# Two contraction tiles of the first tokens by plain loads and TensorE transposes, the other three by one DMA transpose, with all loads on SyncE's queue

## The chip, the core and the metric

The kernel runs on one core of a Trainium2 chip. The metric is device time in microseconds (us), as the median of several executions. The profile that is quoted is of one execution, taken by the hardware profiler; its span runs from the first to the last instruction of the program.

## What is computed

A feed-forward block without biases, all in bf16, with accumulation in float32:

```python
B, S, D, F = 1, 2048, 640, 1728
# x: (B, S, D), w1: (D, F), w2: (F, D)
h = jnp.einsum("bsd,df->bsf", x, w1)
h = silu(h)
out = jnp.einsum("bsf,fd->bsd", h, w2)
```

## The kernel before

TensorE contracts over the 128 partitions. The first product has its contraction over D = 640, which makes five contraction tiles, numbered 0 to 4. F = 1728 is thirteen blocks of 128 columns and a last one of 64. The 2048 tokens are four chunks of 512. The first product is made transposed, with w1 as the stationary operand and x, transposed to `xT` (features on partitions, tokens along the row), as the moving one, so each matmul of a block and a chunk is 128x512 and fills one of the eight PSUM banks after five contraction tiles. ScalarE applies SiLU from PSUM into `hT`. The second product takes `hT` as its operand, most of it with w2 moving; its results are evicted by VectorE and ScalarE in turn and stored by SP. The 64 last columns of F, and the last 128 columns of D in the second product, have paths of their own late in the kernel.

The program is written engine by engine, with semaphores by hand: `wait` puts a wait on an engine ahead of its next instruction, `tick` lets an instruction raise a semaphore. Each engine keeps the order in which the code issues to it. `ahead_of_start` moves what it issues ahead of the barrier at the program's start, and `barrier_wait_here` moves an engine's wait at that barrier to the place of the call. So the order of the first microseconds is that of the code, per engine.

What matters here is chunk 0, the first 512 tokens:

- x must reach `xT` transposed. `turned` does that with a DMA transpose from HBM, `first(i)` for the pairs of tiles in `KT`, which is tiles 1 and 2, and then 3 and 4. Tile 0 goes another way: `xk` is loaded as it stands (tokens on partitions), TensorE transposes its four 128x128 blocks against `ident` into banks 6 and 7, and VectorE copies them to `xT`.
- w1 comes in slabs. `load_k` (called by `slab`) loads the first `FA` = 8 blocks of one contraction tile, 256 KB; `half` loads half of such a slab. Slabs of tiles 0 and 1 come as halves. ScalarE's queue issues two of the four halves, after it has waited for the first two dummies. All other loads are SP's. Blocks 8 to 12 and the last 64 columns follow in two loads for all five tiles (`FG`).
- `dummies` are matmuls on zeros in bank 3: nine ahead of the transposes and one behind them.
- `k_pass(k, fts, a, e)` runs contraction tile k over the blocks `fts`. For chunk 0 the loop over k is outside and that over the eight blocks inside, so eight banks are open at once, and tile k needs only its own part of x and its own slab. Tile 0 starts with four blocks in half width (256 tokens each).
- The blocks from 8 on, and chunks 1 to 3, have the loop over k inside. Their x comes by DMA transposes of two, two and one tile, behind the start's loads in SP's queue.

In the profile every matmul through `mm`, in both products, has line L221. Plain loads and stores are L89, DMA transposes of x L122, dummies L146, TensorE's transposes L195, the copies out of them L197, SiLU L225.

Of the kernel before, what the change touches and what calls it, by code (L numbers as in the profile page):

```python
# [9 lines left out]
def bass_standalone__dense_activation_silu__prompt_kernel(  # L10
# [6 lines left out]
    bf16 = mybir.dt.bfloat16  # L17
# [6 lines left out]
    P = 128  # L24
    NB = 8
    BANK = 512
    DT = D // P
    FT = F // P
    FL = F - FT * P
    SCH = 512  # L30
    HB = 256
# [6 lines left out]
    pe, act, dve, pool, sp = nc.tensor, nc.scalar, nc.vector, nc.gpsimd, nc.sync  # L38

    with ExitStack() as es:  # L40
        def sb(name, shape, dtype):
            return es.enter_context(nc.sbuf_tensor(name, shape, dtype))

        xT = sb("xT", [P, DT, S], bf16)
# [4 lines left out]
        hTt = sb("hTt", [P, NSC // 2, SCH], bf16)  # L49
        oT = sb("oT", [P, S], bf16)  # L50
        o_sb = sb("o_sb", [P, S // P, D], bf16)
        xk = sb("xk", [P, SCH // P, P], bf16)
        ident = sb("ident", [P, P], bf16)
        warm = sb("warm", [P, 32], fp32)
        z = sb("z", [P, HB], bf16)
        ps = es.enter_context(nc.psum_tensor("ps", [P, NB, BANK], fp32))
# [4 lines left out]
        def sem(name):  # L61
            s = es.enter_context(nc.semaphore(name))
            count[s.name if hasattr(s, "name") else name] = 0
            return [s, 0]

        def tick(ins, s, n=1):
            ins.then_inc(s[0], n)
            s[1] += n
            return (s, s[1])

        def wait(eng, *points):
            for pt in points:
                if pt is None:
                    continue
                s, v = pt
                key = (id(eng), id(s))
                if seen.get(key, 0) < v:
                    eng.wait_ge(s[0], v)
                    seen[key] = v

        s_pe, s_act, s_dve = sem("s_pe"), sem("s_act"), sem("s_dve")
# [4 lines left out]
        def load(eng, out_ap, in_ap):  # L86
            s = sem(f"s_ld{n_dma[0]}")
            n_dma[0] += 1
            return tick(eng.dma_start(out=out_ap, in_=in_ap), s, 16)  # L89

        ET = mybir.EngineType

        def preamble(engine, opcode):
            lst = nc.main_func.blocks[0].instructions
            return next(
                i for i, ins in enumerate(lst)
                if ins.opcode == opcode and ins.engine == engine
            )

        def ahead_of_start(emit, engine):  # L100
            lst = nc.main_func.blocks[0].instructions
            n = len(lst)
            r = emit()
            lst = nc.main_func.blocks[0].instructions
            new = lst[n:]
            del lst[n:]
            at = preamble(engine, "Drain")
            lst[at:at] = new
            return r

        def barrier_wait_here(engine):
            lst = nc.main_func.blocks[0].instructions
            lst.append(lst.pop(preamble(engine, "EventSemaphore")))
# [4 lines left out]
        FA = 8  # L118
        FG = [(8, 11), (11, FT)]

        def turned(c, k0, k1, s):
            return tick(sp.dma_start_transpose(  # L122
                out=xT[:, k0:k1, c * SCH:(c + 1) * SCH],
                in_=xf[c * SCH:(c + 1) * SCH, k0 * P:k1 * P],
            ), s, 16)

        def load_k(eng, k):
            return load(eng, w1s[:, k, 0:FA * P], w1_v[:, k, 0:FA * P])

        ld_w1 = {}  # L130
        KT = [(1, 3), (3, DT)]
        s_x = [sem(f"s_x{k0}") for k0, _ in KT]
        ld_x = {}

        def first(i):
            k0, k1 = KT[i]
            pt = turned(0, k0, k1, s_x[i])
            for k in range(k0, k1):
                ld_x[k] = pt
        p_z = ahead_of_start(lambda: tick(dve.memset(z[:, :], 0.0), s_dve), ET.DVE)  # L140
        x_v = xf.rearrange("(j p) d -> p j d", p=P)
        bank_free = [None] * NB

        def dummies(n):
            for _ in range(n):
                ins = pe.matmul(ps[:, 3, 0:HB], lhsT=z[:, 0:P], rhs=z[:, :], start=True, stop=True)  # L146
            return tick(ins, s_pe)
# [9 lines left out]
        FH = FA // 2  # L157
        ld_k = {}

        def slab(k):  # L160
            ld_k[k] = load_k(sp, k)

        def half(eng, k, h):
            a, b = (0, FH * P) if h == 0 else (FH * P, FA * P)
            return load(eng, w1s[:, k, a:b], w1_v[:, k, a:b])

        p_ident = ahead_of_start(identity, ET.Pool)
        ld_xk = ahead_of_start(lambda: load(sp, xk[:, :, :], x_v[:, 0:SCH // P, 0:P]), ET.SP)
        ld_a = {}
        ld_a[0] = ahead_of_start(lambda: half(sp, 0, 0), ET.SP)  # L170
        wait(pe, p_z)
        wait(act, dummies(2))
        ld_k[0] = half(act, 0, 1)
        ld_a[1] = half(act, 1, 0)
        ahead_of_start(lambda: first(0), ET.SP)
        ld_k[1] = ahead_of_start(lambda: half(sp, 1, 1), ET.SP)
        ahead_of_start(lambda: slab(2), ET.SP)
        first(1)
        slab(3)
        slab(4)  # L180
        for a, b in FG:
            e = F if b == FT else b * P
            pt = load(sp, w1s[:, :, a * P:e], w1_v[:, :, a * P:e])
            for ft in range(a, b):
                ld_w1[ft] = pt
        barrier_wait_here(ET.SP)
        barrier_wait_here(ET.Activation)

        dummies(7)
        wait(pe, ld_xk, p_ident)  # L190
        turned0 = []
        for h in range(2):
            v = ps[:, 6 + h, :].bitcast(bf16)
            for i in range(2):
                ins = pe.transpose(v[:, i * P:(i + 1) * P], xk[:, 2 * h + i, :], ident[:, :])  # L195
            wait(dve, tick(ins, s_pe))
            r = tick(dve.tensor_copy(  # L197
                out=xT[:, 0, h * HB:(h + 1) * HB], in_=v[:, 0:HB]), s_dve)
            bank_free[6 + h] = r
            turned0.append(r)  # L200
        dummies(1)
        barrier_wait_here(ET.DVE)

        p_warm = tick(pool.memset(warm[:, :], 0.0), s_pool)
# [15 lines left out]
        def mm(o, l, r, start, stop, shared=False):  # L220
            return pe.matmul(o, lhsT=l, rhs=r, start=start, stop=stop, skip_group_check=shared)  # L221

        def silu(out_ap, in_ap, bank, after):
            wait(act, after)
            r = tick(act.activation(out=out_ap, in_=in_ap, func=ACT.Silu), s_act)  # L225
            bank_free[bank] = r
            return r

        def k_pass(k, fts, a=0, e=SCH):
            for ft in fts:  # L230
                if k == 0:
                    wait(pe, bank_free[ft])
                ins = mm(ps[:, ft, a:e], w1s[:, k, ft * P:(ft + 1) * P], xT[:, k, a:e],
                         start=(k == 0 and a == 0), stop=(k == DT - 1), shared=True)
                if k == DT - 1:
                    silu(hT[:, ft, 0:SCH], ps[:, ft, :], ft, tick(ins, s_pe))

        wait(pe, ld_a[0], turned0[0])
        k_pass(0, range(FH), 0, HB)
        wait(pe, turned0[1])  # L240
        k_pass(0, range(FH), HB, SCH)
        wait(pe, ld_k[0])
        k_pass(0, range(FH, FA))
        wait(pe, ld_x[1], ld_a[1])
        k_pass(1, range(FH))
        wait(pe, ld_k[1])
        k_pass(1, range(FH, FA))
        barrier_wait_here(ET.PE)
        for k in range(2, DT):
            wait(pe, ld_x[k], ld_k[k])  # L250
            k_pass(k, range(FA))

        nxt = [FA]

        def bank():
            b = nxt[0] % NB
            nxt[0] += 1
            wait(pe, bank_free[b])
            return b

        for ft in range(FA, FT):
            wait(pe, ld_w1[ft])
            b = bank()
            for k in range(DT):
                ins = mm(ps[:, b, :], w1s[:, k, ft * P:(ft + 1) * P], xT[:, k, 0:SCH],
                         start=(k == 0), stop=(k == DT - 1))
            silu(hT[:, ft, 0:SCH], ps[:, b, :], b, tick(ins, s_pe))
        for c in range(1, NSC):
            wait(pe, ld_xc[c])
            for ft in range(FT):  # L270
                b = bank()
                for k in range(DT):
                    ins = mm(ps[:, b, :], w1s[:, k, ft * P:(ft + 1) * P],
                             xT[:, k, c * SCH:(c + 1) * SCH], start=(k == 0), stop=(k == DT - 1))
                h_last = silu(hT[:, ft, c * SCH:(c + 1) * SCH], ps[:, b, :], b, tick(ins, s_pe))
        h_tail = []
        for q in range(NSC // 2):
            b = bank()
            for k in range(DT):
                for hh in range(2):  # L280
                    c = 2 * q + hh
                    ins = mm(ps[hh * FL:(hh + 1) * FL, b, :], w1s[:, k, F0:F],
                             xT[:, k, c * SCH:(c + 1) * SCH],
                             start=(k == 0), stop=(k == DT - 1), shared=True)
# [85 lines left out]
        for c in range(NSC):  # L370
            b = bank()
# [5 lines left out]
        for q in range(NSC // 2):  # L377
# [6 lines left out]
            for hh in range(2):  # L384
                c = 2 * q + hh
                r = evac(oT[:, c * SCH:(c + 1) * SCH], ps[:, wbank[c], :], wbank[c], tt[hh])
                wait(sp, r)
                st_w[c] = tick(sp.dma_start_transpose(
                    out=o_sb[:, c * JB:(c + 1) * JB, DA:D],
                    in_=oT[:, c * SCH:(c + 1) * SCH],  # L390
# [36 lines left out]
```

## Time and profile before

| What | us |
|---|---|
| median of 6 runs | 125.22 |
| lowest and highest run | 124.79, 125.67 |
| the profiled execution | 125.17 |
| its span | 123.8 |
| TensorE matmuls, busy | 120.0 |
| TensorE weight loads, busy | 55.1 |
| ScalarE, busy | 38.1 |
| VectorE, busy | 8.1 |

The page lists, for each group of instructions, its line, engine, operation and tiles (out<-in), how many there are, their busy time, the mean time of one in ns, and the idle time of the engine ahead of them with what ended most of it. PE is TensorE's matmuls, PEld its weight loads, DVE VectorE, ACT ScalarE, POOL GpSimd; an engine with a q behind it is its queue, which issues DMAs. Matmuls are pipelined, so that the time of one is longer than the distance between the starts of two.

### The profile page before, as it was taken

The page shows a single profiled execution, that of the slowest core. Times are in us where ns is not written, and L with a number is a line of the kernel's source. Part 1 is how long each engine was busy: PE and PEld are TensorE (multiplying, and loading weights), DVE is VectorE, ACT ScalarE, POOL GpSimd, SP SyncE. Part 2 cuts the span into 40 slices and gives each one's busy share as a digit, 9 for nine tenths or more (in the row PEclk, how much of TensorE's full clock was granted, in tenths as well). Part 3 has the DMA queues.
Part 4 walks back from the last instruction along what each step waited for, and adds up shares of the span by engine and source line. Part 5 has one row for each costly group of instructions (what it writes and reads, how often), then busy time and mean ns, then how long its engine had stood idle before and what let it go on. Part 6 is the DMA issues. An engine that isn't in the chain of part 4 may idle for free.

```text
span 123.8 us, 1349 instructions
## 1 busy us (share of the span) xinstructions
PE 120.0 (97%) x581; PEld 55.1 (44%) x592; DVE 8.1 (7%) x14; ACT 38.1 (31%) x66; POOL 0.8 (1%) x7
## 2 busy tenths in 40 slices
PE   8898999999999999999999999999999999999993
PEld 5434444444444444444434444444434444444452
DVE  1000000000000000000002020200012120102021
ACT  0401975555555555555530101010011101010100
POOL 2000000000000000000000000000000000000000
DMA  5999895999100000000000000000003377111113
GB/s 130 258 326 252 178 160 104 166 285 394 54 0 0 0 5 0 3 0 0 0 0 5 0 0 0 0 0 0 0 0 81 52 232 287 53 53 53 53 53 106
DMA packets 19557, 10.35 MB, mean 84 GB/s; under 512 B 13536, under 2 KB 19168, under 8 KB 19552
## 3 DMA queue, kind: packets, MB, share of 16 engines
q1 hardware_dynamic: 19264, 10.01, 31.6%
q10 hardware_dynamic: 288, 0.26, 1.0%
q8 instruction: 4, 0.07, 0.3%
q14 instruction: 1, 0.01, 0.0%
HBM read 4.64 MB, written 2.62 MB: 59 GB/s over the span
## 4 chain that ended last, share of the span: by engine, by line
PE 90%; SPq 4%; DMA 4%; issue 1%; ACT 0%
PE ps L221 90%; DMA w1s<-in_w_dram 4%; SPq L122 2%; SPq L89 2%; ACT o_sb L296 0%; SPq L412 0%
## 5 line engine op out<-in xcount | busy, mean ns | idle before, releaser
L221 PE MATMUL ps<-xT,w1s 128*128 128x512 bf16 (+2 forms) x279 | 58.6, 376 | 1.2 <-DMA xT<-in_x_dram 0.5
L221 PE MATMUL ps<-w2s,hT 128*128 128x512 bf16 (+2 forms) x216 | 45.0, 366 | 0.4 <-issue 0.2
L221 PEld LDWEIGHTS ps<-xT,w1s 128*128 128x128 bf16 (+1 forms) x284 | 26.6, 99 | 33.1 <-DMA xT<-in_x_dram 1.0
L225 ACT ACTIVATE hT<-ps 128x512 bf16<-128x512 f32 x52 | 30.0, 608 | 26.0 <-PE ps L221 26.0
L221 PEld LDWEIGHTS ps<-w2s,hT 128*128 128x128 bf16 x221 | 20.9, 98 | 24.5 <-issue 1.1
L296 ACT CAST o_sb<-ps 128x512 bf16<-128x512 f32 (+1 forms) x8 | 4.4, 545 | 42.2 <-PE ps L221 42.2
L294 DVE CAST o_sb<-ps 128x512 bf16<-128x512 f32 (+1 forms) x9 | 6.1, 677 | 97.5 <-PE ps L221 95.2
L221 PE MATMUL ps<-hT,w2s 128*128 128x512 bf16 x51 | 11.3, 379 | 0.1
L221 PEld LDWEIGHTS ps<-hT,w2s 128*128 128x128 bf16 x52 | 5.1, 98 | 6.1
L296 ACT CAST oT<-ps 128x512 bf16<-128x512 f32 x2 | 1.1, 588 | 11.0 <-PE ps L221 11.0
L146 PE MATMUL ps<-z 128*128 128x256 bf16 x10 | 2.5, 418 | 0.4 <-DVE z L140 0.4
L206 ACT ACT_TABLE_LOAD x1 | 1.3, 1283 | 3.9 <-DVEq L412 3.9
L221 PE MATMUL ps<-w2t,hTt 64*128 64x512 bf16 (+2 forms) x17 | 2.2, 366 | 0.0
L294 DVE CAST oT<-ps 128x512 bf16<-128x512 f32 x2 | 1.3, 686 | 13.7 <-PE ps L221 13.7
L146 PEld LDWEIGHTS ps<-z 128*128 128x128 bf16 x10 | 1.3, 144 | 0.8 <-DVE z L140 0.4
L225 ACT ACTIVATE hTt<-ps 128x512 bf16<-128x512 f32 x2 | 1.2, 597 | 1.1 <-PE ps L221 1.1
L221 PEld LDWEIGHTS ps<-w2t,hTt 64*128 64x128 bf16 x17 | 0.7, 94 | 1.4 <-issue 0.8
L197 DVE COPY xT<-ps 128x256 bf16<-128x256 bf16 x2 | 0.5, 292 | 2.5 <-PE ps L195 2.5
L195 PE MATMUL ps<-ident,xk 128*128 128x128 bf16 x4 | 0.6, 308 | 0.0
L221 PE MATMUL ps<-hTt,w2t 64*128 64x512 bf16 x4 | 0.6, 381 | 0.0
L195 PEld LDWEIGHTS ps<-ident,xk 128*128 128x128 bf16 x4 | 0.3, 131 | 0.4 <-DMA xk<-in_x_dram 0.4
L221 PEld LDWEIGHTS ps<-hTt,w2t 64*128 64x128 bf16 x4 | 0.1, 94 | 0.4 <-issue 0.4
(9 smaller groups left out, 1.4 us busy)
## 6 DMA issues: line engine op xcount, KB each, us to landing
out_dram<-o_sb SPq DMA_DIRECT2D x15, 160.0 KB, 1.9
w2s<-in_w_dram SPq DMA_DIRECT2D x1, 1120.0 KB, 6.1
w2s<-in_w_dram SPq DMA_DIRECT2D x1, 960.0 KB, 8.2
w1s<-in_w_dram SPq DMA_DIRECT2D x3, 256.0 KB, 4.5
w1s<-in_w_dram SPq DMA_DIRECT2D x1, 480.0 KB, 5.4
w1s<-in_w_dram SPq DMA_DIRECT2D x1, 400.0 KB, 6.1
w1s<-in_w_dram SPq DMA_DIRECT2D x2, 128.0 KB, 3.2
w1s<-in_w_dram ACTq DMA_DIRECT2D x2, 128.0 KB, 3.3
```

The lines of the kernel that those rows point to most:

```text
L89: return tick(eng.dma_start(out=out_ap, in_=in_ap), s, 16)
L122: return tick(sp.dma_start_transpose(out=xT[:, k0:k1, c * SCH:(c + 1) * SCH], in_=xf[c * SCH:(c + 1) * SCH, k0 * P:k1 * P],), s, 16)
L146: ins = pe.matmul(ps[:, 3, 0:HB], lhsT=z[:, 0:P], rhs=z[:, :], start=True, stop=True)
L195: ins = pe.transpose(v[:, i * P:(i + 1) * P], xk[:, 2 * h + i, :], ident[:, :])
L197: r = tick(dve.tensor_copy(out=xT[:, 0, h * HB:(h + 1) * HB], in_=v[:, 0:HB]), s_dve)
L206: act.activation(out=warm[:, :], in_=warm[:, :], func=ACT.Silu)
L221: return pe.matmul(o, lhsT=l, rhs=r, start=start, stop=stop, skip_group_check=shared)
L225: r = tick(act.activation(out=out_ap, in_=in_ap, func=ACT.Silu), s_act)
L294: r = tick(dve.tensor_copy(out=out_ap, in_=in_ap), s_dve)
L296: r = tick(act.copy(out=out_ap, in_=in_ap), s_act)
```

## The change

Tile 1 of chunk 0 goes the way of tile 0: `xk` has room for two tiles, both are loaded as they stand, TensorE makes eight transposes (into banks 6, 7, 4 and 5) and VectorE four copies. Tiles 2, 3 and 4 come by one DMA transpose instead of two. The two half slabs that ScalarE issued are issued by SP; tile 0's slab stays in two halves, that of tile 1 is one load. SP's order at the start is: x columns of tile 0, x columns of tile 1, the two halves of slab 0, slab 1, the transpose of three tiles, slab 2, slab 3, slab 4, and then as before. All nine dummies stand ahead of the transposes and none behind them. TensorE makes the transposes of both tiles before it starts tile 0. Its wait at the barrier stays behind tile 1.

```diff
-        xk = sb("xk", [P, SCH // P, P], bf16)
+        xk = sb("xk", [P, 2, SCH // P, P], bf16)
...
-        KT = [(1, 3), (3, DT)]
+        KT = [(2, DT)]
...
         p_ident = ahead_of_start(identity, ET.Pool)
-        ld_xk = ahead_of_start(lambda: load(sp, xk[:, :, :], x_v[:, 0:SCH // P, 0:P]), ET.SP)
-        ld_a = {}
-        ld_a[0] = ahead_of_start(lambda: half(sp, 0, 0), ET.SP)
-        wait(pe, p_z)
-        wait(act, dummies(2))
-        ld_k[0] = half(act, 0, 1)
-        ld_a[1] = half(act, 1, 0)
+
+        def load_xk(k):
+            return load(sp, xk[:, k, :, :], x_v[:, 0:SCH // P, k * P:(k + 1) * P])
+
+        ld_xk = [ahead_of_start(lambda: load_xk(k), ET.SP) for k in range(2)]
+        ld_k0a = ahead_of_start(lambda: half(sp, 0, 0), ET.SP)
+        ld_k[0] = ahead_of_start(lambda: half(sp, 0, 1), ET.SP)
+        ahead_of_start(lambda: slab(1), ET.SP)
         ahead_of_start(lambda: first(0), ET.SP)
-        ld_k[1] = ahead_of_start(lambda: half(sp, 1, 1), ET.SP)
         ahead_of_start(lambda: slab(2), ET.SP)
-        first(1)
         slab(3)
         slab(4)
+        wait(pe, p_z)
...
-        dummies(7)
-        wait(pe, ld_xk, p_ident)
-        turned0 = []
-        for h in range(2):
-            v = ps[:, 6 + h, :].bitcast(bf16)
-            for i in range(2):
-                ins = pe.transpose(v[:, i * P:(i + 1) * P], xk[:, 2 * h + i, :], ident[:, :])
-            wait(dve, tick(ins, s_pe))
-            r = tick(dve.tensor_copy(
-                out=xT[:, 0, h * HB:(h + 1) * HB], in_=v[:, 0:HB]), s_dve)
-            bank_free[6 + h] = r
-            turned0.append(r)
-        dummies(1)
+        dummies(9)
+        ready = {}
+        for k in range(2):
+            wait(pe, ld_xk[k], p_ident)
+            for h in range(2):
+                b = 6 - 2 * k + h
+                v = ps[:, b, :].bitcast(bf16)
+                for i in range(2):
+                    ins = pe.transpose(v[:, i * P:(i + 1) * P], xk[:, k, 2 * h + i, :], ident[:, :])
+                wait(dve, tick(ins, s_pe))
+                bank_free[b] = ready[k, h] = tick(dve.tensor_copy(
+                    out=xT[:, k, h * HB:(h + 1) * HB], in_=v[:, 0:HB]), s_dve)
...
-        wait(pe, ld_a[0], turned0[0])
+        wait(pe, ld_k0a, ready[0, 0])
         k_pass(0, range(FH), 0, HB)
-        wait(pe, turned0[1])
+        wait(pe, ready[0, 1])
         k_pass(0, range(FH), HB, SCH)
         wait(pe, ld_k[0])
         k_pass(0, range(FH, FA))
-        wait(pe, ld_x[1], ld_a[1])
-        k_pass(1, range(FH))
-        wait(pe, ld_k[1])
-        k_pass(1, range(FH, FA))
-        barrier_wait_here(ET.PE)
-        for k in range(2, DT):
-            wait(pe, ld_x[k], ld_k[k])
+        wait(pe, ready[1, 0], ready[1, 1])
+        for k in range(1, DT):
+            wait(pe, ld_x.get(k), ld_k[k])
             k_pass(k, range(FA))
+            if k == 1:
+                barrier_wait_here(ET.PE)
```

## The prediction

> **What bounds the kernel now.** I read four views in this order: the chain that ended last (what sets the end), the waits cut into two stretches of time (where TensorE stands still), the timelines of TensorE and of SP's queue for the first microseconds, and the DMA rate window by window. First the chain of waits; columns are start, length, what:
>
> ```profile
> 4.95 0.04 issue
> 5.00 4.53 DMA w1s<-in_w_dram
> 9.53 0.14 issue
> 9.66 1.67 PE ps L221 x7
> 11.33 0.05 issue
> 11.38 10.74 PE ps L221 x49
> ...
> 122.02 0.27 ACT o_sb L296
> ```
>
> From 9.66 us to the last eviction the chain is TensorE without a break; before it stands a DMA that landed at 9.53. So the end is set by the moment from which TensorE runs unbroken, and only the first 10 us can move it. The waits confirm it, the first three rows from the stretch 3.2 to 13.2 us, the last the only TensorE wait from 13.2 us to the end:
>
> ```profile
> PEld ps L221 <- DMA xT<-in_x_dram: 1.0, 1, 1.0
> PEld ps L221 <- issue: 0.8, 1, 0.8
> PE ps L221 <- DMA w1s<-in_w_dram: 0.3, 1, 0.3
> ...
> PE ps L221 <- issue: 0.2, 1, 0.2
> ```
>
> TensorE's timeline (start, busy time, what):
>
> ```profile
> 0.38 2.10 PE L146 MATMUL ps<-z 128*128 128x256 bf16 x9 [0.38 <-DVE z L140]
> 2.37 0.61 PE L195 MATMUL ps<-ident,xk 128*128 128x128 bf16 x4
> 2.77 0.42 PE L146 MATMUL ps<-z 128*128 128x256 bf16 x1
> 3.30 1.91 PE L221 MATMUL ps<-xT,w1s 128*128 128x256 bf16 x12
> 5.69 3.63 PE L221 MATMUL ps<-xT,w1s 128*128 128x512 bf16 x16 [0.47 <-DMA xT<-in_x_dram]
> 9.66 2.53 PE L221 MATMUL ps<-xT,w1s 128*128 128x512 bf16 x10 [0.34 <-DMA w1s<-in_w_dram]
> ```
>
> The chain's x49 in 10.74 us gives 0.216 us per 128x512 matmul, so eight of them (one contraction tile over eight banks) are 1.73 us. Tile 0 (8 half-width, 4 full) occupies 3.30 to 5.05, tiles 1 and 2 occupy 5.69 to 9.15, tiles 3 and 4 occupy 9.66 to 13.11. Two holes: 0.64 us for the transposed x of tiles 1 and 2, and 0.51 us for the weight slab of tile 3. Together 1.15 us is what a better order of loads can win at most, apart from an earlier start than 3.30.
>
> SP's queue (start, time to issue) and the DMA windows (last two columns: DMA share, GB/s):
>
> ```profile
> 0.00 0.46 SPq L89 DMA_DIRECT2D xk<-in_x_dram  x1
> 0.51 0.49 SPq L89 DMA_DIRECT2D w1s<-in_w_dram  x1
> 1.05 1.32 SPq L122 DMA_TRANSPOSE xT<-in_x_dram  x1
> 2.42 1.05 SPq L89 DMA_DIRECT2D w1s<-in_w_dram  x2
> 3.71 1.24 SPq L122 DMA_TRANSPOSE xT<-in_x_dram  x1
> ...
> 2.00:3.00 1.00, 1.00 (x8) 0.46 (x6) 0.20 (x1) 0.00 (x0) 0.00 (x0) 1.00 0.86 205
> 4.00:5.00 1.00, 1.00 (x8) 0.46 (x5) 0.00 (x0) 1.00 (x1) 0.00 (x0) 1.00 1.27 212
> 5.50:6.00 0.50, 0.31 (x2) 0.20 (x3) 0.00 (x0) 0.00 (x0) 0.00 (x0) 1.00 1.00 389
> 6.25:6.75 0.50, 0.50 (x4) 0.20 (x2) 0.00 (x0) 0.00 (x0) 0.00 (x0) 1.00 1.28 291
> ```
>
> The DMA engines are busy without a pause from about 1.3 us (share about 1), at 205 to 219 GB/s between 2 and 5 us, 389 while a 256 KB weight slab runs alone, 291 while the second x transpose runs alone. So the start is bound by bytes and their order, not by TensorE.
>
> **The change part by part.**
>
> *Start of real work.* Removed: the tenth dummy, the two ACT-issued half slabs and ACT's wait for two dummies. Added: a second 128 KB load of x columns, four transposes, two copies. The nine dummies keep their place to 2.28 us. The first x load landed 2.32 after its issue; the second is issued 0.51 later and queued behind it. At about 250 GB/s its 131 KB need 0.5 us, so I take 2.8 for its landing. Its four transposes (four took from 2.37 to 2.79, 0.107 each) stand in TensorE's order before the first real matmul: done at 3.25. The first half slab is now third in SP's queue; it had landed at 3.26 while sharing the engines with ACT's half slab, and now has 131 KB more before it and nothing beside it: 3.3. Start about 3.35, against 3.30. Bounds: 3.2 if the start-up is kinder, 3.75 if the second x load needs the 2.75 us that the second load needed before. The copies (292 ns) now take banks 4 and 5 too, which tile 0 first writes 0.87 us after the start; done by then, so nothing.
>
> *Tiles 0 and 1.* Tile 0 needs 1.74 us: 3.35 to 5.09. Its second half slab and the whole slab of tile 1 follow in SP's queue and should land near 4.0 and 4.8. Tile 1 no longer waits for a DMA transpose and runs 5.09 to 6.81. That is where the 0.64 us hole goes. What is late next is tile 2: it needs the one transpose of tiles 2 to 4 and slab 2, both now behind it in the queue.
>
> *The three-tile transpose.* SP issues 0.46+0.46+0.49+0.52+0.45 us of plain loads, with 0.05 between, so the transpose is issued from about 2.65 instead of 1.05. Issuing took 1.24 to 1.32 for two tiles, so I take 1.32 for three: done at 3.97. It moves 1536 pieces of 256 B. At the 291 GB/s of the row that is 1.35 us; with a ramp as after an empty queue, 1.55. Slab 2 (262 KB, 0.67 us at 389) is behind it.
>
> *When slab 2 lands.* Two ways. Sum of stages: both x loads 1.2 to 2.3 us, two half slabs at the 205 of the start-up row 1.3 us to 3.6, slab 1 0.75 to 4.35, transpose 1.55 to 5.9, slab 2 0.7 to 6.6, and about 0.6 from the last byte to the semaphore (slab 2 before: last byte near 6.06, landed 6.69): 7.2. By bytes: 1.44 MB have to pass up to slab 2, against 1.15 MB before; the windows of before reach 1.44 MB at 7.0, so 7.6. The difference is whether the 205 to 219 GB/s came from the mixture of two queues with 256 B pieces, or is simply what the start yields. Here the row is weighed against the Trainium skill, DMA: Bandwidth & Descriptors, "Issuing engines are not separate DMA queues": DMAs of all issuers share the same engines and interleave, and a second issuer saves only issue time. By that rule unmixing gains nothing, slab 2 lands at 7.6 and the change wins little. The rows say that plain slabs alone run at 389 and transposes alone at 291, and only the mixed stretch is slow, so I go most of the way to the sum of stages: 7.25.
>
> A second rule speaks against the change itself. Advanced Engine Details and Errata, "X-Bar Transpose (TRN2)", has transposing DMAs as fast as regular ones, 350 to 400 GB/s. Then the three tiles would take 1.05 us, slab 2 would land at 6.8, but a tile moved to plain loads would save no transfer time and only add TensorE work. The 6.25 to 6.75 row has 291, and the measured row decides; the rule is used for the good end of the range.
>
> *Tiles 2 to 4.* Tile 2 starts at 7.25 (before: 7.43) and ends at 8.98. Slabs 3 and 4 are no longer behind a second transpose; slab 3's bytes end near 7.3, landing near 7.8. Before, it landed at 9.53, 1.3 us later than its neighbours' pace: one of its sixteen parts was late. If that repeats it lands near 9.2 and costs 0.2; in the likeliest case I have it in time. Tiles 3 and 4 then end at 8.98 + 3.45 = 12.43, against 13.11: 0.7 us earlier, 0.5 with a late part.
>
> *At no cost.* SP's drain, which releases the barrier, moves from 3.52 to about 4.5, so ACT's table load (1.28 us) moves from 3.87 to about 4.85. The first activation is not due before 10.8; without that cover it would cost about a microsecond. TensorE's barrier wait comes after tile 1, 6.8 us, long released. The last two weight loads have the same bytes before them as now (landed 11.5 and 12.7) and are due at 12.4 and 15.7. Chunk 1's transposes landed at 15.54 and are due at 17.9. The tail shifts as a block.
>
> Sum: 125.17 for the profiled run (span 123.8 and 1.4 around it) less 0.7 is 124.5. The median of the runs is 125.22, 0.05 away, so the same number serves. About 0.5% (0.63 us) is what measurement of this kernel can tell from no change.
>
> **The rivals.**
>
> 1. *Bytes bind, the waits only move.* Slab 2 lands at 7.5 to 7.6 by the rule above, tile 2 starts 0.1 later than now, and only part of the 0.51 hole closes: 0 to 0.4 us gained, 124.8 to 125.2. For it: the DMA share is about 1 already and 0.26 MB of x have moved ahead of slab 2. Against it: the pure stretches are faster.
>
> 2. *The three-tile transpose runs at the pace of the first one.* The first transpose, in the mixed stretch, needed about 2.25 us for two tiles. At that pace three need 3.4: bytes done at 7.7, slab 2 at 8.4, landed at 8.9. Tile 2 then starts 1.5 later than now, the 0.51 hole is gone, net 1.0 slower: 126.2. It decides from a landing of slab 2 later than 7.43 + 0.51 = 7.94. A late part of slab 2 as in slab 3 before has the same place and price (8.6: 0.6 slower). For it: one transpose now gates three tiles with no spare time. Against it: nothing on another queue runs beside it now.
>
> 3. *The clock of TensorE.* Dummies of 256 columns start 0.21 apart, the real ones 0.11 apart: the full rate arrived just before 3.30. The skill's TensorE: Matmul & The Clock Gate, Part 1, calls the window free-running, so it may come later in other runs. Before, the holes hid that; now a microsecond at half rate on tiles 0 and 1 costs up to 0.5 less the 0.44 by which tile 1 ends before slab 2 lands. 124.5 to 125.0.
>
> **How the numbers follow.** Forecast, with its better side: 0.47, of which 0.04 lies within the bound. Rivals 1 and 3: 0.29, nearly all within the bound. Rival 2 with its late-part form: 0.24 slower. Faster 0.43, same 0.33, slower 0.24. The good end, both holes closed, is 125.17 - 1.15 = 124.0, with 0.1 for an earlier start 123.9; the upper end goes most of the way to rival 2: 126.0.
>
> **What would show it.** Right: the first L221 matmul at 3.2 to 3.5, no hole between tiles 0 and 1, a hole of 0.3 to 0.5 before tile 2 that ends with slab 2 near 7.25, and tile 4's end near 12.4. Wrong: a transpose with over 2.2 us of traffic, slab 2 past 7.6, or first real matmuls 0.2 apart at half width.

## The result, and the profile after

The changed kernel is slower: 125.79 us median of 21 runs (125.24 to 127.46), against 125.17 us for the kernel before over 42 runs on the same chips (124.79 to 125.70). The ratio is 1.005, 95% interval 1.0034 to 1.0066. Medians are of all runs; the ratios here and below leave out the few that were over 1.5% above the fastest of their kernel. The forecast was 124.5. The execution profiled first took 125.28 (span 124.0), at the lower end of its runs, so I took the trace of the same kernel twice more: 126.49 and 125.84.

The chain of waits of the first trace (start, length, what), where before the chain turned to TensorE at 9.66 with a weight slab ahead of it:

```profile
2.54 1.57 SPq L122
4.11 0.05 issue
4.16 3.76 DMA w1s<-in_w_dram
7.91 0.14 issue
8.05 2.75 PE ps L220 x12
10.80 0.05 issue
10.85 10.74 PE ps L220 x49
```

There is again one slab of weights in the chain, but it is slab 2 now, issued behind the three-tile transpose, and not slab 3. It landed at 7.91, and tile 2 starts at 8.05 (7.43 before). Lines that were L195, L197, L221 and L225 are L197, L199, L220 and L224 in the changed kernel. TensorE's timeline:

```profile
0.39 2.10 PE L146 MATMUL ps<-z 128*128 128x256 bf16 x9 [0.39 <-DVE z L140]
2.40 1.33 PE L197 MATMUL ps<-ident,xk 128*128 128x128 bf16 x8
3.71 3.90 PE L220 MATMUL ps<-xT,w1s 128*128 128x256 bf16 x20
8.05 6.20 PE L220 MATMUL ps<-xT,w1s 128*128 128x512 bf16 x27 [0.43 <-DMA w1s<-in_w_dram]
```

The waits of TensorE's matmuls and weight loads between 3.2 and 13.4 us:

```profile
PEld ps L220 <- issue: 0.9, 1, 0.9
PE ps L220 <- DMA w1s<-in_w_dram: 0.4, 1, 0.4
PEld ps L197 <- DMA xk<-in_x_dram: 0.4, 1, 0.4
PEld ps L220 <- DMA w1s<-in_w_dram: 0.2, 1, 0.2
```

Both old holes are gone, and no matmul waits for a DMA transpose of x any more. In their place the real work starts 0.4 later (3.71, not 3.30), tiles 0 and 1 run as one block, and one hole stands ahead of tile 2. The last two rows lie ahead of the real work: the transposes of tile 1 wait for the second x load (landed at 3.08), and the first real weight load, at 3.70, waits for the first half slab (landed at 3.66). The second trace of the same kernel has the same picture with a hole of 1.65 us, the third has none:

```profile
3.74 4.04 PE L220 MATMUL ps<-xT,w1s 128*128 128x256 bf16 x20
9.26 4.91 PE L220 MATMUL ps<-xT,w1s 128*128 128x512 bf16 x21 [1.49 <-DMA w1s<-in_w_dram]
```

```profile
3.66 10.51 PE L220 MATMUL ps<-xT,w1s 128*128 128x256 bf16 x45
```

The third has no hole because TensorE itself was slow. Its chain of waits is TensorE alone from the first real matmul on, and no weight slab stands in it:

```profile
3.66 119.02 PE ps L220 x577
```

The matmuls by form between 3.2 and 7.5 us (busy, mean ns of one), first in the first trace, then in the third, and the half-width ones of the kernel before:

```profile
L220 PE MATMUL ps<-xT,w1s 128*128 128x512 bf16 x12 | 2.8, 379 | 0.0
L220 PE MATMUL ps<-xT,w1s 128*128 128x256 bf16 x8 | 1.3, 318 | 0.0
```

```profile
L220 PE MATMUL ps<-xT,w1s 128*128 128x512 bf16 x7 | 2.4, 494 | 0.0
L220 PE MATMUL ps<-xT,w1s 128*128 128x256 bf16 x8 | 1.9, 415 | 0.0
```

```profile
L221 PE MATMUL ps<-xT,w1s 128*128 128x256 bf16 x8 | 1.0, 274 | 0.1
```

The starts of successive matmuls are 0.213 us apart at half width while TensorE runs at half rate, and 0.109 after; in the three traces the short distance, the full rate, begins at 4.3, 4.7 and 6.9 us, before by 3.4.

| trace | first real matmul | tile 1 ends | slab 2 lands | tile 2 starts | time |
|---|---|---|---|---|---|
| changed, first | 3.71 | 7.45 | 7.91 | 8.05 | 125.28 |
| changed, second | 3.74 | 7.61 | 9.12 | 9.26 | 126.49 |
| changed, third | 3.66 | 8.61 | 8.34 | 8.61 | 125.84 |

From tile 2 to the end nothing differs: each of the three times is 117.23 us more than the start of tile 2. Two things gate that start, slab 2 and TensorE's own pace, and the later of them decides: slab 2 in the first two traces, TensorE in the third.

The DMA side. SP's queue of the changed kernel, and the DMA windows (last two columns: share, GB/s), the last row being the mean of the first seven microseconds:

```profile
1.04 1.45 SPq L89 DMA_DIRECT2D w1s<-in_w_dram  x3
2.54 1.57 SPq L122 DMA_TRANSPOSE xT<-in_x_dram  x1
4.16 2.66 SPq L89 DMA_DIRECT2D w1s<-in_w_dram  x5
```

```profile
3.50:4.00 0.50, 0.50 (x5) 0.24 (x3) 0.44 (x2) 0.00 (x0) 0.00 (x0) 1.00 0.76 154
5.50:6.00 0.50, 0.50 (x4) 0.26 (x3) 0.00 (x0) 0.50 (x1) 0.00 (x0) 1.00 1.27 290
0.00:7.00 7.00, 6.49 (x35) 3.78 (x36) 1.17 (x5) 1.51 (x2) 0.76 (x7) 1.00 0.88 209
```

The same row of the kernel before:

```profile
0.00:7.00 7.00, 6.03 (x33) 3.35 (x34) 0.67 (x3) 1.51 (x2) 0.76 (x7) 1.00 0.90 205
```

209 against 205 GB/s: the new order of loads moved no more bytes in that time. The column ahead of the DMA share is the granted clock. It reads 1.00 in every row, also where the starts lie at the double distance, so it does not show this half rate.

### The profile page after: what moved, and what is told of

Same layout as the page of the kernel before. It is cut to its first block, busy times and chain, and to the rows that moved or that the text cites. A ratio compares the mean times of both kernels' runs of the same rounds, so it can differ in the third digit from the quotient of the medians.

```text
span 124.0 us, 1356 instructions
## 1 busy us (share of the span) xinstructions
PE 120.5 (97%) x584; PEld 55.6 (45%) x595; DVE 8.6 (7%) x16; ACT 38.1 (31%) x66; POOL 0.8 (1%) x7
## 4 chain that ended last, share of the span: by engine, by line
PE 91%; SPq 3%; DMA 3%; issue 1%; ACT 0%
PE ps L220 91%; DMA w1s<-in_w_dram 3%; SPq L89 2%; SPq L122 1%; ACT o_sb L293 0%
## 5 line engine op out<-in xcount | busy, mean ns | idle before, releaser
L220 PE MATMUL ps<-xT,w1s 128*128 128x512 bf16 (+2 forms) x279 | 58.7, 377 | 0.7 <-DMA w1s<-in_w_dram 0.4
L220 PE MATMUL ps<-w2s,hT 128*128 128x512 bf16 (+2 forms) x216 | 45.0, 366 | 0.4 <-issue 0.2
L220 PEld LDWEIGHTS ps<-xT,w1s 128*128 128x128 bf16 (+1 forms) x284 | 26.9, 99 | 32.3 <-issue 0.9
L224 ACT ACTIVATE hT<-ps 128x512 bf16<-128x512 f32 x52 | 30.0, 608 | 24.9 <-PE ps L220 24.9
L220 PEld LDWEIGHTS ps<-w2s,hT 128*128 128x128 bf16 x221 | 20.9, 98 | 24.4 <-issue 1.1
L220 PE MATMUL ps<-hT,w2s 128*128 128x512 bf16 x51 | 11.3, 379 | 0.1
L220 PEld LDWEIGHTS ps<-hT,w2s 128*128 128x128 bf16 x52 | 5.1, 98 | 6.1
L220 PE MATMUL ps<-w2t,hTt 64*128 64x512 bf16 (+2 forms) x17 | 2.2, 366 | 0.0
L224 ACT ACTIVATE hTt<-ps 128x512 bf16<-128x512 f32 x2 | 1.2, 597 | 1.1 <-PE ps L220 1.1
L220 PEld LDWEIGHTS ps<-w2t,hTt 64*128 64x128 bf16 x17 | 0.7, 94 | 1.4 <-issue 0.8
L197 PE MATMUL ps<-ident,xk 128*128 128x128 bf16 x8 | 1.2, 307 | 0.1
L199 DVE COPY xT<-ps 128x256 bf16<-128x256 bf16 x4 | 1.0, 292 | 2.7 <-PE ps L197 2.7
L197 PEld LDWEIGHTS ps<-ident,xk 128*128 128x128 bf16 x8 | 0.7, 130 | 0.8 <-DMA xk<-in_x_dram 0.8
L220 PE MATMUL ps<-hTt,w2t 64*128 64x512 bf16 x4 | 0.6, 381 | 0.0
L220 PEld LDWEIGHTS ps<-hTt,w2t 64*128 64x128 bf16 x4 | 0.1, 94 | 0.4 <-issue 0.4
```

Source lines behind the costliest of these rows:

```text
L197: ins = pe.transpose(v[:, i * P:(i + 1) * P], xk[:, k, 2 * h + i, :], ident[:, :])
L199: bank_free[b] = ready[k, h] = tick(dve.tensor_copy(out=xT[:, k, h * HB:(h + 1) * HB], in_=v[:, 0:HB]), s_dve)
```

## The experiments

Ratios are to the kernel before, run in turn on the same chip; its medians there were 125.14 to 125.32.

### Is it slab 2?

A second trace of the changed kernel (a2_again), without an edit.

> The changed kernel once more, for a second trace, as its first profiled run (125.28) lay 0.5 under the median of its runs. In four traces with the same order of loads (the changed kernel, e1_fill, e4_late, e5_late_fill) slab 2 landed at 7.9, 8.4, 8.4 and 8.5 us. Theory 'late slab 2': it lands at 8.2 to 8.6 here too, tile 2 starts with it, and the time is about 125.8. Theory 'clock': slab 2 is in time and the half rate lasts past 5 us.

Measured: 126.49; slab 2 landed at 9.12, later than expected, and tile 2 started with it (shown above). In the trace a load is counted in by sixteen completions: fifteen of slab 2's came by 7.94, the last at 9.12; in the first trace fourteen came by 7.47, the last at 7.91. So most of the delay is one late part. The bulk was 0.47 later too. The DMA traffic had sunk for a while, by about 122 KB, which is 0.4 us at 290 GB/s (an estimate from the two rows and the 290 above). The windows from 5.00 to 5.75 us of the first trace and of the second:

```profile
5.00:5.75 0.75, 0.75 (x6) 0.32 (x4) 0.00 (x0) 0.63 (x1) 0.12 (x1) 1.00 1.18 257
5.00:5.75 0.75, 0.75 (x6) 0.30 (x4) 0.00 (x0) 0.12 (x1) 0.11 (x1) 1.00 0.98 94
```

A third trace (a3_again):

> The changed kernel a third time. Slab 2, directly behind the three-tile transpose, lands at 8.2 to 9.2, later than the 7.94 from which the change loses, and tile 2 starts with it; the time is 125.6 to 126.5 according to that landing.

Measured: 125.84; slab 2 at 8.34 (fifteen parts by 7.54), but TensorE, at half rate to 6.9, ended tile 1 only at 8.61, and tile 2 followed without a hole. Landing and time fell where they were expected, but the cause that I had named was not the one: without the late part this run would have taken as long.

**Slab 2 ahead of the transpose** (e7_swap):

```diff
-        ahead_of_start(lambda: first(0), ET.SP)
         ahead_of_start(lambda: slab(2), ET.SP)
+        ahead_of_start(lambda: first(0), ET.SP)
```

> The changed kernel with slab 2 issued ahead of the transpose of three tiles. The bytes that tile 2 needs are the same. Theory 'bytes': the transpose now lands last, near 7.5 to 7.9, tile 2 starts there, and slab 3 follows it: 125.4 to 125.8. Theory 'the slab behind the transpose comes late in parts': slab 2 is now out of its way, tile 2 starts near 7.6, and the late part hits slab 3, which has a microsecond to spare: 125.2 to 125.4. If a transpose of all parts waits for the slowest of them, nothing is gained: 125.8 or more.

Measured: 125.39, ratio 1.0008 (0.9994 to 1.0022). Its interval lies wholly under that of the changed kernel, 1.0034 to 1.0066: exchanging two lines takes the loss away here (e10_swap_fill below, with the same exchange, is still 0.2% over the kernel before). Slab 2 landed at 6.48, the transpose at 8.00. In its trace nothing waits for either, since TensorE was at half rate to 6.2:

```profile
0.51 2.75 DMA xk<-in_x_dram
3.27 0.05 issue
3.31 0.61 PE ps L197 x4
3.92 7.19 PE ps L220 x32
11.11 0.05 issue
```

The chain goes from the second x load through TensorE's transposes straight into the matmuls, without a weight slab.

**Nobody waits for slab 2** (e8_noslab2):

```diff
-                ins = mm(ps[:, ft, a:e], w1s[:, k, ft * P:(ft + 1) * P], xT[:, k, a:e],
+                ins = mm(ps[:, ft, a:e], w1s[:, 1 if k == 2 else k, ft * P:(ft + 1) * P], xT[:, k, a:e],
...
-            wait(pe, ld_x.get(k), ld_k[k])
+            wait(pe, ld_x.get(k), ld_k[1 if k == 2 else k])
```

> The changed kernel in which tile 2 of the first tokens multiplies with slab 1's weights, so that no matmul waits for slab 2; slab 2 is still loaded, so all transfers stay. What is left out is the right weights of that tile. Theory 'late slab 2' (its landing at 7.9 to 8.5 is where the time goes): tile 2 starts when tile 1 ends or the transpose lands, at 7.0 to 7.5, tile 3 at about 9.1 with slab 3, and the time falls by 0.4 or more, to 125.0 to 125.4. Theory 'clock' or 'start': no change, 125.8.

Measured: 125.42, ratio 1.0013 (0.9991 to 1.0036), with a profiled run of 125.83 that was at half rate to 6.6 and had no hole. The median is as expected from "late slab 2", though the interval still touches that of the changed kernel (from 1.0034). In the one trace TensorE's rate sets the pace; whether it makes the rest of the spread is not shown.

### Is it the queue?

**The kernel before with all loads on SP** (b1_queue):

```diff
-        wait(act, dummies(2))
-        ld_k[0] = half(act, 0, 1)
-        ld_a[1] = half(act, 1, 0)
+        dummies(2)
+        ld_k[0] = ahead_of_start(lambda: half(sp, 0, 1), ET.SP)
+        ld_a[1] = ahead_of_start(lambda: half(sp, 1, 0), ET.SP)
```

> The kernel before with its two half slabs of ScalarE's queue issued by SP, in the order x, half slab, two half slabs, transpose of tiles 1 and 2, and on. Only the queue changes. Theory 'queue' (the queue and the later issue of the first transpose are what the change loses by): the first transpose is issued 1 us later, at 2.1, and lands at 6.2 or later instead of 5.64; tile 1 starts 0.5 later and the time rises by 0.2 to 0.5, to 125.4 to 125.7. Theory 'three tiles ahead of slab 2': no change, within 0.2 of the kernel before.

Measured: 126.06, ratio 1.0065 (1.0041 to 1.0089), more than expected. The first transpose landed at 5.90, 0.3 later than before. Most of the loss is in the hole ahead of tile 3, behind the second transpose:

```profile
4.66 1.24 SPq L122
5.89 0.04 issue
5.93 4.16 DMA w1s<-in_w_dram
```

Slab 3, issued at 5.93, landed at 10.10, with thirteen parts by 9.54. That could be the queue (all of it was issued a microsecond later than before) or the slab's place.

**The same with slab 3 ahead of the second transpose** (b4_queue_swap):

```diff
-        first(1)
         slab(3)
+        first(1)
         slab(4)
```

> The kernel before with all loads on SP (b1_queue, 126.06) and slab 3 ahead of the second DMA transpose. Theory 'late slab': b1_queue lost through slab 3, which landed at 10.1 behind the second transpose and left a hole of 0.8 us, and not through the queue as such; with the swap the time falls by 0.5 or more, to 125.2 to 125.5. Theory 'queue' (SP alone issues too late and fills the engines less): it stays at 125.8 to 126.1.

Measured: 125.16, ratio 1.0000 (0.9987 to 1.0013). The whole loss of b1_queue goes. Moving ScalarE's loads to SP need not cost time; it cost when a slab behind a transpose came late. It does move fewer bytes: in the first seven microseconds 178 GB/s in b1_queue against 205 in the kernel before, and 185 here against 202 in b3_swap (below), which differs from this kernel in the queue alone. The row of b1_queue:

```profile
0.00:7.00 7.00, 6.28 (x31) 3.47 (x32) 0.67 (x3) 1.51 (x2) 0.76 (x7) 1.00 0.81 178
```

**The changed kernel with the two half slabs on ScalarE's queue** (e3_actq):

```diff
-        ld_k[0] = ahead_of_start(lambda: half(sp, 0, 1), ET.SP)
-        ahead_of_start(lambda: slab(1), ET.SP)
+        wait(pe, p_z)
+        wait(act, dummies(2))
+        ld_k[0] = half(act, 0, 1)
+        ld_k1a = half(act, 1, 0)
         ahead_of_start(lambda: first(0), ET.SP)
+        ld_k[1] = ahead_of_start(lambda: half(sp, 1, 1), ET.SP)
...
-        dummies(9)
+        dummies(7)
...
-        wait(pe, ready[1, 0], ready[1, 1])
+        wait(pe, ready[1, 0], ready[1, 1], ld_k1a)
```

> The changed kernel with the two half slabs back on ScalarE's queue, behind the first two dummies, as in the kernel before. Theory 'queue' (one queue alone fills the DMA engines worse in the first microseconds, and the three-tile transpose is issued 1 us later for the loads ahead of it): the transpose is issued at about 1.5 instead of 2.5 us, slab 2 lands 0.5 us or more earlier, the time falls to about 125.2. Theory 'late loads' by bytes: slab 2 lands at the same time within 0.3 us, since the same bytes pass; the time stays within 0.2 of 125.8.

Measured: 126.88, ratio 1.0127 (1.0105 to 1.0148). Slab 2 did land earlier, at 7.26, as the theory "queue" had it (224 GB/s in the first seven microseconds, against 209, 191 and 208 in the traces of the changed kernel). But the second x load came at 3.62 and the first half slab at 4.43, with ScalarE's loads beside them. TensorE's timeline:

```profile
3.67 0.61 PE L199 MATMUL ps<-ident,xk 128*128 128x128 bf16 x4 [0.65 <-DMA xk<-in_x_dram]
4.48 9.84 PE L222 MATMUL ps<-xT,w1s 128*128 128x256 bf16 x42 [0.20 <-DMA w1s<-in_w_dram]
```

From 4.48 it never waits again, but it is at half rate to 7.5. Neither theory had this later start: I had priced the end of the loads and forgotten their beginning.

### Is it TensorE's rate?

**Dummies in the gaps** of the changed kernel (e1_fill): `dummies(2 - k)` at the end of the loop over the two tiles' transposes.

> The changed kernel with three more dummies: two between the transposes of tile 0 and of tile 1, one behind those of tile 1, so that TensorE has no idle gap ahead of the first real matmul. Theory 'clock': in the changed kernel TensorE stands idle three times before its first real matmul, its first three real matmuls ran at half rate, and in other runs the full rate comes later still, which makes the upward tail of its times. Then the time falls to about 125.3 and the tail over 126 goes away, and all half-width real matmuls start 0.11 apart. Theory 'late loads' (slab 2 and the three-tile transpose decide when tile 2 starts, whatever TensorE does before): no change, about 125.8, with tile 2 again starting near 8.0 us.

Measured: 126.08, ratio 1.007 (1.0042 to 1.0098). Full rate came at 4.0, yet the time did not fall: slab 2 landed at 8.44 and tile 2 started at 8.58. The dummies also put the start off, to 3.87. So curing the rate alone does not take the loss away.

**TensorE's transposes of tile 1 behind the half-width part of tile 0** (e4_late), the loop body made a function `turn(k)`:

```diff
         k_pass(0, range(FH), HB, SCH)
+        turn(1)
+        barrier_wait_here(ET.DVE)
         wait(pe, ld_k[0])
```

> The changed kernel with TensorE's transposes of tile 1 behind the half-width matmuls of tile 0, so that the first real matmul waits for the first half slab alone. Theory 'late loads': the first real matmul comes no more than 0.1 us earlier, as the half slab landed at 3.66 in the changed kernel, and tile 2 starts as before near 8.0: no change, about 125.8. Theory 'start' (the transposes ahead of the first real matmul are what costs): 0.4 us faster, about 125.4.

Measured: 126.63, ratio 1.013 (1.0095 to 1.0166). The start was 3.62, 0.1 earlier, as expected; the slowdown was not expected. TensorE stood idle for 0.9 us ahead of it, and ran at half rate to 7.3. The edit has a second cost: tile 1's transposes now stand between the halves of tile 0, and their results lie in banks 4 and 5, which tile 0's second half (blocks 4 to 7) writes next. So that half waits for the copy out of bank 4 (done at 6.05), 0.9 us after the first half:

```profile
6.20 8.00 PE L222 MATMUL ps<-xT,w1s 128*128 128x512 bf16 x34 [0.26 <-DVE xT L200]
```

Tile 1 ended at 9.28, long after slab 2 (8.35). The next experiment, e6_order and e9_two have the same gap, of 0.75 to 0.9 us.

**The same with four dummies in that gap** (e5_late_fill): `dummies(4)` behind `turn(0)`.

> The kernel with the late transposes of tile 1 (e4_late) and four dummies added behind the transposes of tile 0, which fill the 0.9 us for which TensorE stood idle ahead of its first real matmul; nothing else differs. Theory 'clock' (idle time ahead of the real matmuls puts off the full rate): the full rate comes near 4 us instead of 7.3, tile 1 ends before the loads of tile 2 have landed, and the time falls from 126.6 to 125.8, where the loads bind. Rival (the full rate comes at a random time in any kernel and the idle gap is no cause): the times stay near 126.6.

Measured: 126.62, ratio 1.0093 (1.0061 to 1.0126), the eight runs between 125.47 and 128.83. The trace is of one of the faster runs, 125.91. What the dummies do to the rate is plain; the half-width matmuls of e4_late, then of e5_late_fill:

```profile
L222 PE MATMUL ps<-xT,w1s 128*128 128x256 bf16 x8 | 1.9, 418 | 0.7 <-DMA w1s<-in_w_dram 0.7
```

```profile
L223 PE MATMUL ps<-xT,w1s 128*128 128x256 bf16 x8 | 1.0, 274 | 0.0
```

But tile 2 waited for slab 2 to 8.67, and what the median should have gained cannot be told in that spread. The median of 125.8 that I expected was missed.

**The kernel before with five dummies instead of nine** (b2_gap): `dummies(3)` for `dummies(7)`.

> The kernel before with five dummies instead of nine ahead of the transposes, so that TensorE stands idle from 1.45 to 2.37 us. The loads are untouched. Theory 'clock': the full rate comes later than 5 us, tile 0 takes 3.5 us instead of 1.75 and its cover, two holes of 1.15 us, is overrun: 125.8 to 126.5. Rival (idle time of a microsecond does nothing to the rate): no change, 125.2.

Measured: 125.57, ratio 1.0042 (1.0022 to 1.0061). Half rate lasted to 6.1, no hole was left, and 0.4 us were lost in the median: the holes of the kernel before cover most of a slow start, and I had priced their cover too low.

**Both causes taken out of the changed kernel** (e10_swap_fill): the exchange of e7_swap and the dummies of e1_fill.

> The changed kernel with slab 2 ahead of the three-tile transpose (e7_swap, 125.39) and the three dummies of e1_fill. In e7_swap's trace TensorE ran at half rate to 6.2 us and had no hole, so the rate and not the loads set its pace. Theory 'clock': with the idle gaps filled the full rate comes near 4 us, tile 2 starts when the transpose lands (7.7 to 8.0), and the time falls by 0.1 to 0.4, to 125.0 to 125.3. If the transpose's landing binds at 8.0 either way: no change, 125.4.

Measured: 125.40, ratio 1.0023 (1.0008 to 1.0038), no better than e7_swap. Full rate came at 3.9, and the three-tile transpose binds instead:

```profile
3.02 4.89 DMA xT<-in_x_dram
7.91 0.05 issue
7.96 2.12 PE ps L221 x9
```

In the two traces with this order of bytes the transpose landed at 8.00 and 7.91, so tile 2 could not start before that, half a microsecond later than in the kernel before (7.43).

### Other orders

**The three-tile transpose split** (e2_split), `KT = [(2, 3), (3, DT)]` with `first(1)` behind slab 2:

> The changed kernel with the transpose of three tiles split: tile 2 alone ahead of slab 2, tiles 3 and 4 behind it. Theory 'late loads': slab 2 has 262 KB less ahead of it and lands 0.9 us earlier, near 7.0; tile 2 starts when tile 1 ends (near 7.4), and the time falls by 0.4 to 0.6, to about 125.2 to 125.4, unless slab 3 or 4 is now the late one, as one more issue of 1.3 us stands ahead of them. Theory 'clock': no change in the median and the tail stays.

Measured: 125.77, ratio 1.0035 (1.0018 to 1.0053). Slab 2 landed at 7.55, not 7.0, and slab 3, behind the second transpose now, at 9.79. TensorE at half rate to 5.7 hid the first of them. Mostly a miss.

**First half slab ahead of the second x load, with late transposes, two dummies and the split** (e6_order):

> A version put together from the parts: the first half slab ahead of the second x load, late transposes of tile 1, two dummies behind the transposes of tile 0, and tile 2's transpose alone ahead of slab 2. All loads on SP. By 'late loads' and 'clock' together the first real matmul comes at 3.3, the full rate near 4, tile 2 starts at 7.5 with slab 2, and slab 3, which has the same bytes ahead of it as before, binds at 9.2 to 9.8: 124.9 to 125.4, equal to the kernel before. If the order of bytes alone is not what binds, it stays over 125.6.

Measured: 125.87, ratio 1.0053 (1.0035 to 1.0071). The start was 3.30 as expected, but tile 0's second half began only at 5.35, behind tile 1's transposes, the copy out of bank 4 (done at 5.21) and the second half slab (5.15), and slab 3 came at 9.76. A miss.

**The kernel before, both queues kept, with tile 1 by a plain load** (e9_two): x of tile 1 behind the first half slab, `KT = [(2, 4), (4, DT)]`, late transposes.

> The kernel before with its two queues kept, and only tile 1 of x changed: loaded as it stands behind the first half slab and transposed on TensorE behind the half-width matmuls of tile 0; the DMA transposes take tiles 2 and 3, and then tile 4. Theory 'queue' (what costs is the move of ScalarE's loads): the plain load of tile 1 then does no harm, 125.0 to 125.4, with tile 1 waiting for ScalarE's second half slab near 5.3. If the second x load is itself the cost (131 KB more ahead of the rest), it is 125.6 or more.

Measured: 125.93, ratio 1.0062 (1.0042 to 1.0082). Tile 0's second half began at 5.85, behind tile 1's transposes and the copy out of bank 4 (done at 5.71), and slab 3, behind the second transpose, landed at 10.58 (fifteen parts by 9.44). The second branch of the expectation fits the number; but the late slab and the gap in tile 0 are in it too, so it does not show that 131 KB more are the cost.

**The kernel before with slab 3 ahead of its second transpose** (b3_swap), the edit of b4_queue_swap:

> The kernel before with slab 3 issued ahead of its second DMA transpose (tiles 3 and 4); nothing else differs. Theory 'the slab queued directly behind a transpose lands late in one or two of its sixteen parts': slab 3 is out of its way and lands near 7.4 to 7.6 instead of 9.53, the transpose lands near 8.3, before tile 3 is due at 9.15, and the late part falls on slab 4, which is due at 10.9. The second hole (0.51 us) goes: 124.6 to 124.9. If lateness goes with slab 3 or with the time of about 7 to 9 us, and not with the place behind a transpose, the transpose or slab 3 is late all the same and it stays at 125.2.

Measured: 125.07, ratio 0.9994 (0.9982 to 1.0006). Slab 3 landed at 7.60, all parts within 0.06 us, the transpose at 8.69, and tile 3 followed tile 2 without a hole, as expected. The expected 0.3 to 0.6 us did not come: no measurable gain. A second trace of the kernel before tells why (b0_again):

> The kernel before once more, for a second trace. b3_swap took slab 3 out of its place behind the second transpose and gained nothing measurable (0.9994). If the hole of 0.5 us ahead of tile 3 is typical of the kernel before, slab 3 lands at 9.3 or later here too, and b3_swap must have lost the gain elsewhere. If it was a single case, slab 3 lands by 9.2 and tile 3 follows tile 2 without a hole.

Measured: 124.77, slab 3 at 9.08 with fifteen parts by 8.36, and no hole ahead of tile 3: its chain is TensorE without a break from the start of tile 1.

```profile
5.79 115.81 PE ps L221 x565
```

The hole of 0.51 us was one execution's; b2_gap, with the same loads, had slab 3 at 8.58. No version here beats the kernel before by a measurable amount.

## Why the prediction was wrong

The step that failed is the start of tile 2. The forecast had it at 7.25, as the landing of slab 2, with TensorE done with tile 1 at 6.81 and waiting; it came at 8.05, 9.26 and 8.61. In the first two traces the landing of slab 2 was mis-sized, in the third the pace of tiles 0 and 1. And most of the gain that was counted in behind tile 2 was not there to be had. All three signs of being wrong that the prediction names came: over 2.2 us of traffic for the transpose (2.4 in the second trace), slab 2 past 7.6, and first real matmuls 0.21 apart.

*What held.* The constants: 1.73 us a tile and 5.17 from tile 2's start to the end of tile 4 fit every trace. Tile 1 no longer waited for a transpose. ScalarE's table load moved to 5.12 and cost nothing; the later weight loads, chunk 1 and the tail moved as a block. The last byte counts held in the first and third traces: 1.44 MB had passed by about 7 us (for the kernel before, the same addition gives 1.18 MB up to slab 2, not 1.15; nothing rests on it).

*Start of real work.* 3.35 was forecast, 3.66 to 3.74 measured, next to the upper bound of 3.75. The term at fault is the landing of the first half slab, 3.3 in the sum and 3.66, 3.69 and 3.62 in the three traces: the first real weight load follows it by 0.04 each time. The second x load was late as well (2.8 in the sum, 2.99 to 3.25 measured), but its transposes were done at about 3.53, 3.69 and 3.44, ahead of that landing in the first and third traces and together with it in the second. e4_late, which takes them out of the way, starts only 0.1 earlier, again with the half slab.

*Tiles 0 and 1.* They were summed at full rate, 6.81 for the end of tile 1; measured 7.45, 7.61 and 8.61. That is rival 3, which I priced as up to 0.5 for a microsecond at half rate, nearly covered by the wait for slab 2. Half rate lasted up to 3.2 us in the real work. All the traces, ordered by how long TensorE stood idle between its first dummy and its first real matmul (worked out from the starts of its matmuls; e9_two is left out, since a wait hides when its rate changed):

| idle ahead of the real work, us | traces | full rate from, us |
|---|---|---|
| 0.1 to 0.25 | e1_fill, e5_late_fill, e6_order, e10_swap_fill | 3.8 to 4.3 |
| 0.3 to 0.4 | kernel before (two), b3_swap, b4_queue_swap | 3.3 to 4.4 |
| 0.55 to 0.7 | changed kernel (three), e2_split, e7_swap, e8_noslab2, b1_queue | 4.3 to 6.9 |
| 0.9 to 1.4 | b2_gap, e3_actq, e4_late | 6.1 to 7.5 |

So the dropped dummy and the wait for the second x load put the changed kernel where the full rate comes late in some runs and not in others. The kernel before scatters too, by a microsecond between its two traces.

*When slab 2 lands.* 7.25 was forecast; 7.91, 9.12 and 8.34 measured. The step had two estimates and I took the wrong one: its bulk was in by 7.5, 7.9 and 7.5, which is the estimate by bytes (7.6) and what the Trainium skill's DMA: Bandwidth & Descriptors, "Issuing engines are not separate DMA queues", makes of it. 209 against 205 GB/s over seven microseconds is the row that decides: taking the second queue away did not speed the mixed stretch. The other traces go further: 176 to 209 GB/s in the thirteen with one queue, 189 to 224 in the six with two. The rest, 0.4 to 1.2 us, is the late part that I had given as the second form of rival 2, with the right place and with too small a chance. (Its threshold of 7.94 is that of tile 2's start; the landing comes 0.14 ahead, so the loss begins at 7.80.) Two runs take that wait away in different ways and both bring the kernel near the kernel before: e7_swap clear of the changed kernel's interval, e8_noslab2 just touching it. With e1_fill, which cures the rate and gains nothing, that is what shows slab 2 as the main part of the median's loss.

*The three-tile transpose.* Issuing it took 1.57, 2.08 and 1.60 us, not 1.32, and it landed at 6.79 to 7.24. Where it ran alone its traffic was 290 GB/s, so the price of 291 stands, and the rule of equal speed does not show itself here. But from its first packet to its last it took 2.0, 2.4 and 2.1 us and not 1.55: it began beside slab 1, and in the second trace came the stretch at 94 GB/s. In e8_noslab2 and e4_late, with the same order of loads, that stretch moved 107 and 50 GB/s, and the bulk of slab 2 came at 8.1 and 8.3. The pace of rival 2's main form, 3.4 us, was not reached.

*The gain counted in.* 0.51 us of the 0.7 came from closing the hole ahead of tile 3. b3_swap closes it in the kernel before and gains nothing measurable, and a second trace has no such hole: I took one execution's lateness for a property of the kernel, and the same lateness in the changed kernel for an accident. (I also read one late part of that slab 3; there were two, at 8.85 and 9.53.)

*Open.* Why parts of a slab behind a transpose come late, and how the loss divides over the runs between slab, half rate and the later start: the profile shows a few executions of many, and no run has the later start alone.

## What to carry to other kernels

When a wait ends with the landing of one load, look at its sixteen completions and at a second trace before counting the hole as a gain: the size of a late part belongs to one execution, but how much room a load has behind a transpose is set by the order. Put what is due first ahead of a DMA transpose in its queue, and let what has time to spare stand behind it. Before blaming one wait, see when the engine would have been ready without it: in the third trace the late slab cost nothing. And mind an idle stretch ahead of the first real matmul: taking four dummies away cost 0.4 us (b2_gap). Adding dummies brought the full rate forward but saved no time, as the loads bound then (e1_fill, e10_swap_fill). Holes further on may cover a slow start, so closing them brings it to light.

## What the runs showed of the hardware

- The load directly behind the last of the start's transposes often had a late last part: in 14 of 19 traces its last completion came 0.35 to 2.3 us after its eighth (0.5, 1.2 and 0.8 in the changed kernel, 1.4 and 0.8 in the kernel before), in the other five, b2_gap with the kernel before's order among them, within 0.11. In 13 of the 14 a packet of 2 KB in that stretch took 0.4 to 2.4 us, where the median is 0.08 (at most 0.5 in the other five traces). The lateness is then handed on: in the second trace of the changed kernel the last parts of slabs 2, 3 and 4 came 1.23, 1.27 and 1.22 after the eighth, as if one of sixteen lanes had fallen behind and stayed there. The slab taken out of that place had no late last part in e7_swap, b3_swap and b4_queue_swap; in e7_swap slab 3, now behind the transpose, had one (0.8). The mechanism is not shown.
- TensorE's half rate at the start lasted to between 3.3 and 7.5 us, longer with more idle time ahead of the real work but with much scatter, with the granted clock at 1.00 throughout.
- Issuing a DMA transpose took 1.16 to 1.21 us for one tile and 1.23 to 1.32 for two at the start of these kernels, but 1.50 to 2.34 for three.
